# Pooled sums of v over 112 and 32 keys instead of 72 and 72, and a new hand-written order of all steps

## The chip, the cores and the metric

The kernel runs on one core of a Trainium2 chip. The metric is the device time in microseconds of one execution. Three runs of the kernel before gave 593.35, 593.8 and 591.56 us; the median is 593.35 us.

## The reference

Two stages. Attention over 8 batches of 8 heads, 576 positions of width 64, is the sum of a pooled and a local part; its result is the input of a feed-forward stage over 4608 tokens (512 to 1024 to 512). All is float32.

```python
# pooled: means of 4 neighbours, so 144 pooled queries, keys and values per head
q_d, k_d, v_d = (t.reshape(B, H, 144, 4, D).mean(axis=3) for t in (q, k, v))
out_up = np.repeat(softmax(scale * q_d @ k_d.T) @ v_d, 4, axis=2)
# local: each position sees positions less than 4 away
out_local = softmax(where(|i - j| < 4, scale * q @ k.T, -1e9)) @ v
x = (out_up + out_local).transpose(0, 2, 1, 3).reshape(4608, 512)
# feed-forward
h = x @ w_in
solu = h * softmax(h)
ln = (solu - mean(solu)) / sqrt(var(solu) + 1e-6) * g_ln
out = ln @ w_out
```

## The kernel before

The work is cut into 2039 numbered steps. A step is a stretch of a generator up to its next `yield`, mostly one to twelve instructions on one engine. The list `plan` holds them in a natural order; the string `ORDER` is a permutation of 0 to 2038 written out by hand, and the kernel issues the steps in that order. Each engine runs its instructions strictly in the order in which they are issued, so `ORDER` sets the queue of every engine, SyncE's with its DMAs too. The string `OTHER` lists the steps that go to the second of two engines: `engine(usual, instead)` returns `instead` if the step's number is in it.

The steps, by item:

- `warm` (24 steps, L1042): two matmuls on a constant tile, into the bank that the output of the feed-forward uses later. They only keep TensorE busy.
- Batches 0 and 1 (`EarlyBatch.pair_steps`): TensorE turns q and k around (L556), a copy (L262 or L264), and VectorE sums four neighbours (L418: `qd_flat`, `kd`). Batches 2 to 7 (`Batch.pair_steps`): VectorE transposes (L462, L466) and sums.
- `pooled_vload` and `pooled_vsum`: four loads per batch, each of four heads and half of the pooled keys: 288 positions as 72 partitions of 4 positions each (`vs`, L315), and two additions that make 72 pooled keys in `vd` (L486, L489). They run on GpSimd, or on VectorE for steps in `OTHER`.
- `Pooled` (32 items of 10 steps, one for each pair of heads of a batch): scores (L787), maximum (L794), exponentials (L802), division (L809, L811), twelve transposes of the probabilities by TensorE (L822, into `pdt`: a 64x72 block is the stationary operand, a 64x64 identity is streamed), two copies into `pdT`, the product with `vd` (L843), and the addition into x (L577). The two halves of the 144 keys are `kc` 0 and 1.
- `Local` and `PairOfLocals`: the local part, windows of 64 positions (L606, L694, L654, L664, L752; VectorE L624 to L642 and L700 to L745).
- `Weights.piece` (16 items): w_in and w_out arrive as float64 and are turned into two float32r parts each (L363 to L411).
- For each of 36 tiles of 128 tokens: `xhl` splits x into two parts (L1016, L1019); `ffn_in` makes h by 24 matmuls in two steps (L861), then maximum (L869), exponential (L873), product (L876), mean and spread; `ffn_back` writes u to DRAM and reads it back in blocks; `ffn_ut` transposes and splits it (L962, L968, L971); `ffn_out` makes the output by 24 matmuls in two steps (L985), scales (L992) and stores it (L994). h has one buffer of two PSUM banks and the output one bank, so tile i+1 may start h only after L876 of tile i has read it.

"h of tile 8" below means the first of the two `ffn_in` steps of tile 8 with L861. `PairOfLocals` and the steps in between are placed by `ORDER` alone; no code weighs them at run time.

Of the kernel before, what the change touches and what calls it, by code (L numbers as in the profile page):

```python
# [10 lines left out]
F32 = mybir.dt.float32  # L11
# [125 lines left out]
def pooled_local_attention_then_solu_ffn(  # L137
# [11 lines left out]
    P = 128  # L149
# [17 lines left out]
    starts = [0] + [58 * w - 3 for w in range(1, 9)] + [S - W]  # L167
    qlo = [58 * w for w in range(9)] + [520]
    qhi = qlo[1:] + [S]

    QC = 3
    QN = SD // QC

# [981 lines left out]
```

## Time and profile before

| what | value |
|---|---|
| median of three runs | 593.35 us |
| span of the profiled execution, first to last instruction | 592.8 us |
| TensorE matmul busy | 568.5 us (96%) |
| VectorE busy | 468.1 us (79%) |
| ScalarE busy | 335.9 us (57%) |
| GpSimd busy | 317.8 us (54%) |
| moved by DMA | 99.58 MB |

The profile is one execution; its span is 0.55 us below the median of the three runs. "Busy" is the share of time in which an engine had an instruction in work; TensorE's matmuls overlap one another and their ends are modelled. A line number such as L861 is the line of the kernel before.

### The profile page before, as it was taken

The page shows a single profiled execution, that of the slowest core. Times are in us where ns is not written, and L with a number is a line of the kernel's source. Part 1 is how long each engine was busy: PE and PEld are TensorE (multiplying, and loading weights), DVE is VectorE, ACT ScalarE, POOL GpSimd, SP SyncE. Part 2 cuts the span into 40 slices and gives each one's busy share as a digit, 9 for nine tenths or more (in the row PEclk, how much of TensorE's full clock was granted, in tenths as well). Part 3 has the DMA queues.
Part 4 walks back from the last instruction along what each step waited for, and adds up shares of the span by engine and source line. Part 5 has one row for each costly group of instructions (what it writes and reads, how often), then busy time and mean ns, then how long its engine had stood idle before and what let it go on. Part 6 is the DMA issues. An engine that isn't in the chain of part 4 may idle for free.

```text
span 592.8 us, 15179 instructions
## 1 busy us (share of the span) xinstructions
PE 568.5 (96%) x5832; PEld 439.3 (74%) x5832; DVE 468.1 (79%) x769; ACT 335.9 (57%) x751; POOL 317.8 (54%) x465
## 2 busy tenths in 40 slices
PE   8789799999989999999999999999999999999996
PEld 5567567677767777777777777787787777778885
DVE  6987999999898989887988968978885854654441
ACT  3577677785555655574457455575445645434443
POOL 2475799577765735485366734354532676242211
PEclk9698999999999999999999999999999999999999
DMA  9998779777787688785897858765535454332331
GB/s 272 237 239 168 162 178 201 184 143 210 178 190 179 147 235 183 173 209 169 194 187 186 203 155 156 214 150 177 159 101 159 133 143 139 106 126 90 124 108 53
DMA packets 207112, 99.58 MB, mean 168 GB/s; under 512 B 163136, under 2 KB 193344, under 8 KB 207040
## 3 DMA queue, kind: packets, MB, share of 16 engines
q1 hardware_dynamic: 207040, 98.61, 66.5%
q8 instruction: 46, 0.75, 0.6%
q14 instruction: 26, 0.21, 0.1%
HBM read 65.54 MB, written 27.79 MB: 157 GB/s over the span
## 4 chain that ended last, share of the span: by engine, by line
PE 72%; DVE 10%; SPq 4%; DMA 4%; issue 4%; POOL 3%; ACT 2%; DVEq 0%; POOLq 0%; ACTq 0%
PE h L861 28%; PE o L985 27%; SPq L285 3%; PE sd L787 2%; PE po L843 2%; PE xp L752 2%; PE pdt L822 2%; PE kp L556 2%; PE warm L1042 2%; PE qp L556 1%; PE sc L694 1%; DMA qm<-in_q_dram 1%; DMA u<-e 1%; POOL xl L1019 1%; PE sc L606 1%
## 5 line engine op out<-in xcount | busy, mean ns | idle before, releaser
L861 PE MATMUL h<-wi_h,xh 128*128 128x512 f32 x288 | 116.6, 405 | 0.9 <-DVE e L876 0.7
L985 PE MATMUL o<-wo_h,uh 128*128 128x512 f32 x288 | 116.4, 404 | 0.8 <-ACT uh L968 0.7
L861 PE MATMUL h<-wi_h,xl 128*128 128x512 f32 x288 | 114.3, 397 | 2.6 <-DVE xl L1019 1.4
L985 PE MATMUL o<-wo_l,uh 128*128 128x512 f32 x288 | 113.9, 395 | 0.0
L861 PE MATMUL h<-wi_l,xh 128*128 128x512 f32 x288 | 113.8, 395 | 0.0
L985 PE MATMUL o<-wo_h,ul 128*128 128x512 f32 x288 | 79.0, 395 | 0.0
L869 DVE TENSOR_REDUCE nmx<-h 128x1 f32<-128x1024 f32 x36 | 43.5, 1209 | 36.0 <-PE h L861 36.0
L873 ACT ACTIVATE e<-h,nmx 128x1024 f32<-128x1024 f32 x36 | 40.1, 1113 | 49.8 <-DVE nmx L869 46.0
L861 PEld LDWEIGHTS h<-wi_h,xl 128*128 128x128 f32 x288 | 54.1, 188 | 16.8 <-POOL xl L1019 2.0
L861 PEld LDWEIGHTS h<-wi_h,xh 128*128 128x128 f32 x288 | 54.1, 188 | 16.0 <-DVE e L876 1.9
L985 PEld LDWEIGHTS o<-wo_h,uh 128*128 128x128 f32 x288 | 54.0, 188 | 15.8 <-issue 1.6
L985 PEld LDWEIGHTS o<-wo_h,ul 128*128 128x128 f32 x288 | 54.0, 188 | 13.3 <-DVE ul L971 0.3
L861 PEld LDWEIGHTS h<-wi_l,xh 128*128 128x128 f32 x288 | 54.1, 188 | 12.0
L985 PEld LDWEIGHTS o<-wo_l,uh 128*128 128x128 f32 x288 | 54.1, 188 | 11.9
L971 POOL TENSOR_TENSOR ul<-v,uh 128x512 fp32r<-128x512 f32 x37 | 48.3, 1312 | 24.7 <-ACT uh L968 20.9
L876 DVE SCALAR_TENSOR_TENSOR e<-h,e 128x1024 f32<-128x1024 f32 x36 | 43.7, 1213 | 16.7 <-ACT e L873 16.5
L968 ACT ACTIVATE uh<-v 128x512 fp32r<-128x512 f32 x70 | 42.5, 623 | 21.0 <-DVE v L962 16.9
L962 DVE STREAM_TRANSPOSE v<-v 128x512 f32<-128x512 f32 x70 | 46.6, 688 | 4.8 <-DMA v<-u 4.8
L992 ACT ACTIVATE osb<-o,s 128x512 f32<-128x512 f32 x36 | 24.6, 682 | 43.3 <-PE o L985 18.3
L1019 POOL TENSOR_TENSOR xl<-x,xh 128x512 fp32r<-128x512 f32 (+1 forms) x31 | 37.6, 1219 | 16.5 <-ACT xh L1016 16.0
L881 POOL TENSOR_SCALAR nmu<-su 128x1 f32<-128x1 f32 x36 | 9.8, 273 | 67.0 <-DVE e L876 56.7
L899 ACT ACTIVATE e<-e,nmu 128x1024 f32<-128x1024 f32 x29 | 33.3, 1148 | 19.7 <-POOL nmu L881 19.7
(122 smaller groups left out, 1142.6 us busy)
## 6 DMA issues: line engine op xcount, KB each, us to landing
u<-e SPq DMA_DIRECT2D x35, 512.0 KB
v<-u SPq DMA_DIRECT2D x140, 128.0 KB
vs<-in_v_dram SPq DMA_DIRECT2D x32, 288.0 KB
out_dram<-osb SPq DMA_DIRECT2D x36, 256.0 KB
qm<-in_q_dram SPq DMA_DIRECT2D x96, 72.0 KB
km<-in_k_dram SPq DMA_DIRECT2D x96, 72.0 KB
vw<-in_v_dram SPq DMA_DIRECT2D x80, 64.0 KB
vw<-in_v_dram SPq DMA_DIRECT2D x40, 128.0 KB
```

The costliest lines, as they stand in the source:

```text
L285: nc.sync.dma_start(t[nm][Q * 32:Q * 32 + 32, pr], src[b, 2 * pr + par, :, dh * 32:dh * 32 + 32].rearrange("(k t) d -> t k d", t=32),)
L861: nc.tensor.matmul(hps[:, n, :], src[:, cc, :], wt[:, cc, n * 512:(n + 1) * 512], start=(cc == 0 and src is xh and wt is wi_h), stop=(cc = ...
L869: nc.vector.tensor_reduce(out=nmx, in_=hf, op=ALU.max, axis=AX.X, negate=True)
L873: nc.scalar.activation(e, hf, AF.Exp, bias=nmx, scale=1.0, accum_out=se)
L876: nc.vector.scalar_tensor_tensor(out=e, in0=hf, scalar=1.0, in1=e, op0=ALU.mult, op1=ALU.mult, accum_out=su)
L899: nc.scalar.activation(e, e, AF.Identity, bias=nmu, scale=1.0)
L962: nc.vector.transpose(vg, vg)
L968: nc.scalar.activation(uh, tp, AF.Copy)
L971: (usual if v is None else engine(usual, nc.vector)).tensor_tensor(out=ul, in0=tp, in1=uh.bitcast(F32), op=ALU.subtract)
L985: nc.tensor.matmul(o, src[:, j, :], wt[:, 4 * g + j, :], start=(g == 0 and j == 0 and src is uh and wt is wo_h), stop=(g == 1 and j == 3 a ...
L992: nc.scalar.activation(osb, o, AF.Copy, scale=s)
L1019: engine(nc.gpsimd, nc.vector).tensor_tensor(out=l, in0=src, in1=h.bitcast(F32), op=ALU.subtract)
```

## The change

The 144 pooled keys are cut at 112 (`K0`) instead of 72. Keys 0 to 111 lie on partitions 0 to 111 of `vd[:, 0]`; keys 112 to 143 lie on partitions 96 to 127 of `vd[:, 1]`, and partitions 0 to 95 there are set to zero once, by GpSimd. The loads of v are 112 and 32 partitions high (448 and 128 KB), the additions likewise. The twelve transposes of a `Pooled` item take 128 columns instead of 72: columns 0 to 127 for the first piece and 16 to 143 for the second, whose columns 16 to 111 meet the zeros of `vd`. The copies move the same number of elements per partition on 128 instead of 72 partitions; the products with `vd` contract over 112 and 128 partitions instead of 72. `vd` is one tile for all batches; it was a tile of a pool with one buffer. Code for a way of summing v on TensorE that was switched off (`SUMS_ON_PE = 0`) is removed. The plan of 2039 steps and their numbers stay as they are; `ORDER` is a new permutation of them, and `OTHER` has 118 numbers instead of 115.

```diff
 ORDER = """
-23 16 165 166 2 4 167 168 169 170 171 24 26 27 25 28 29 3 172 33 32 30 31 173 174 197 17 175
...
+12 3 18 173 24 26 174 8 17 165 166 25 175 176 177 178 27 15 179 167 168 169 2 28 170 29 32 30 31
...
+    K0 = 112
...
+    KEYS = ((0, slice(0, K0), slice(0, K0)), (SD - P, slice(K0, SD), slice(P - SD + K0, P)))
+    vd = cpool.tile([P, 2, H, D], F32, name="vd")
+    nc.gpsimd.memset(vd[0:P - SD + K0, 1], 0.0)
+
     def load_vs(b, c, hs):
-        vs = big(f"vs_{b}_{c}_{hs.start}")[0:72].rearrange("p (h x) -> p h x", h=H // 2)
+        _, keys, at = KEYS[c]
+        vs = big(f"vs_{b}_{c}_{hs.start}")[at].rearrange("p (h x) -> p h x", h=H // 2)
         nc.sync.dma_start(
-            vs, v[b, hs, c * 288:(c + 1) * 288, :].rearrange("h (p t) d -> p h (t d)", t=FAC)
+            vs, v[b, hs, FAC * keys.start:FAC * keys.stop, :].rearrange(
+                "h (p t) d -> p h (t d)", t=FAC
+            ),
         )
...
         def value(self, kc, head):
-            return [self.vd[:, kc, head, :]]
+            return [vd[0:(K0, P)[kc], kc, head, :]]
...
-                out=self.vd[:, c, hs], in0=vs[:, :, 0:D], in1=vs[:, :, D:2 * D], op=ALU.add
+                out=vd[KEYS[c][2], c, hs], in0=vs[:, :, 0:D], in1=vs[:, :, D:2 * D], op=ALU.add
...
-            pt = pt[0:72, :, 0:2 * QC * 64].rearrange("p x (k j n) -> p x k j n", k=2, j=QC)
+            pt = pt[:, :, 0:2 * QC * 64].rearrange("p x (k j n) -> p x k j n", k=2, j=QC)
...
-                            pt[:, x, kc, j, :], pd[rows(x), (0, 2, 1)[c], kc * 72:(kc + 1) * 72],
+                            pt[:, x, kc, j, :], pd[rows(x), (0, 2, 1)[c], KEYS[kc][0]:KEYS[kc][0] + P],
                             ident[rows(x), rows(x)],
...
-            pdT = wk.tile([72, 2, QC, 2, QN], F32, tag="pdT", name=f"pdT_{b}_{pr}")
+            pdT = wk.tile([P, 2, QC, 2, QN], F32, tag="pdT", name=f"pdT_{b}_{pr}")
...
                         nc.tensor.matmul(
-                            po[par * 64:par * 64 + 64, :], vt, pdT[:, kc, par * SD:(par + 1) * SD],
+                            po[par * 64:par * 64 + 64, :], vt,
+                            pdT[0:(K0, P)[kc], kc, par * SD:(par + 1) * SD],
```

More of the change, by code (lines that the diff above doesn't have):

```diff
@@ L179, in pooled_local_attention_then_solu_ffn @@
     WARM = 24
-    SUMS_ON_PE = 0
     G_LATE = False
@@ L224, in pooled_local_attention_then_solu_ffn @@
     nc.vector.memset(mhalf, -0.5)
-    GR = SD // 2
-    BAND = {0: (0, 16), 1: (3, 15), 3: (1, 15)}
-    bands = {}
-    def make_bands():
-        t = moe.tile([P, DFF], F32, tag="e", name="bands")[:, 0:3 * 160]
-        t = t.rearrange("p (r x) -> p r x", r=3)
-        nc.gpsimd.memset(t, 0.0)
-        by_half = ident.rearrange("p (h k) -> p h k", h=2)
-        for n, (r, (off, m)) in enumerate(BAND.items()):
-            nc.vector.tensor_reduce(
-                out=t[:, n, GR:GR + m],
-                in_=by_half[:, :, off:off + FAC * m].rearrange("p h (j i) -> p j h i", i=FAC),
-                op=ALU.add, axis=AX.XY,
-            )
-            bands[r] = t[:, n]
     LP = 2 * W + 2
@@ L439, in __getattr__ @@
                 self.kd = att.tile([P, NPR, SD], F32, tag="kd", name=f"kd_{self.b}", bufs=2)
-            elif what == "vd":
-                self.vd = att.tile([72, 2, H, D], F32, tag="vd", name=f"vd_{self.b}")
             else:
@@ L489, in pooled_vsum @@
             eng.tensor_tensor(
-                out=self.vd[:, c, hs], in0=vs[:, :, 0:D], in1=vs[:, :, D:2 * D], op=ALU.add
+                out=vd[KEYS[c][2], c, hs], in0=vs[:, :, 0:D], in1=vs[:, :, D:2 * D], op=ALU.add
             )
-        def pool_steps(self):
-            firsts = [-(-s0 // FAC) for s0 in starts]
-            ends = firsts[1:] + [SD]
-            for c in range(2):
-                tp = two_banks(ps_h, "h", f"vp_{self.b}_{c}")[0:GR]
-                at = tp.rearrange("p h (r a d) -> p h r a d", r=NPR, a=2)
-                ws = range(5 * c, 5 * c + 5)
-                for w in ws:
-                    s0, g0, g1 = starts[w], firsts[w], ends[w]
-                    at0 = GR - (g0 - GR * c)
-                    K = FAC * g1 - s0
-                    for half in range(2):
-                        nc.tensor.matmul(
-                            at[:, half, :, half ^ (w % 2), :],
-                            bands[s0 % FAC][half * W:half * W + K, at0:at0 + GR],
-                            self.vw[w // 2][half * W:half * W + K, w % 2],
-                            start=w == ws[0], stop=w == ws[-1],
-                        )
-                yield
-                vd = self.vd[:, c].rearrange("p h d -> p (h d)")
-                nc.scalar.activation(vd, tp[:, 0], AF.Copy)
-                yield
-                nc.vector.tensor_tensor(out=vd, in0=vd, in1=tp[:, 1], op=ALU.add)
-                yield
     class EarlyBatch(Batch):
@@ L1076, in attention @@
     def attention(bt):
-        by_pe = bt.b < SUMS_ON_PE
         late = bt.b == 0
@@ L1083, in attention @@
         pooled = [Pooled(bt, pr, late) for pr in range(NPR)]
-        if by_pe:
-            if not bt.b:
-                step(make_bands)
-            for u in range(5):
-                step(bt.load_v, u)
-            row(bt.pool_steps(), 6)
-        else:
-            values(bt)
+        values(bt)
         for it in pooled + local if late else local + pooled:
@@ L1097, in attention @@
                 continue
-            if isinstance(it, Local) and not by_pe:
+            if isinstance(it, Local):
                 step(bt.load_v, it.u)
```

202 rows, old and new, of tables (ORDER, OTHER) are left out of this document.

## The prediction, made before the changed kernel was run

> **What bounds the kernel now.** I read the page's busy totals first, then the chain that ended last, then busy time by stage. Columns of a stage: stretch and length in us, then busy us of TensorE's matmuls, its weight loads, VectorE, ScalarE and GpSimd with the instructions of each, granted clock, DMA share, GB/s.
>
> ```profile
> PE 568.5 (96%) x5832; PEld 439.3 (74%) x5832; DVE 468.1 (79%) x769; ACT 335.9 (57%) x751; POOL 317.8 (54%) x465
> ...
> PE 72%; DVE 10%; SPq 4%; DMA 4%; issue 4%; POOL 3%; ACT 2%; DVEq 0%; POOLq 0%; ACTq 0%
> ```
>
> ```profile
> 0.00:60.00 60.00, 49.77 (x778) 36.19 (x782) 48.24 (x88) 35.94 (x92) 29.24 (x36) 0.86 0.96 228
> 60.00:185.10 125.10, 116.82 (x1530) 87.96 (x1519) 119.48 (x202) 83.85 (x190) 92.53 (x109) 1.00 0.79 180
> 185.10:592.80 407.70, 401.90 (x3540) 315.15 (x3540) 300.41 (x481) 216.15 (x471) 196.04 (x321) 1.00 0.59 155
> ```
>
> ```profile
> 183.92 0.80 DVE e L876
> 185.07 3.07 PE h L861 x12
> ...
> 194.01 5.60 PE o L985 x24
> 199.61 5.60 PE h L861 x24
> ```
>
> 96% says TensorE, but the stages differ. Up to 185.1 us VectorE has the upper hand: between 60 and 185.1 us it is busy 119.48 of 125.1 us, and the chain (start, length, engine, result, line) steps from VectorE to TensorE at h of tile 8. From there the chain is almost TensorE alone, with 401.90 of 407.7 us busy. So the time is two sums: when h of tile 8 or 9 can start (VectorE's work ahead of it plus VectorE's holes), and TensorE's work from there to the end. VectorE's holes before 185.1 us are 11.76 + 5.62 = 17.4 us. Loads matter at the start, where the DMA engines are 0.96 busy; later at 0.59 to 0.79 they are not the bound.
>
> **The transposes of the probabilities.** Each of the 32 `Pooled` items has twelve; their stationary operand grows from 72 to 128 columns. Rows: line, engine, result and operands, weights by moving tile, count, then busy us and mean ns of one.
>
> ```profile
> L822 PE MATMUL pdt<-ident,pd 64*72 64x64 f32 x384 | 16.9, 224 | 0.0
> ...
> L654 PE MATMUL plt<-ident,pl 128*128 128x128 f32 x80 | 12.9, 283 | 2.2 <-POOL pl L644 1.5 <-ACT plT L262 0.7
> ...
> L822 PEld LDWEIGHTS pdt<-ident,pd 64*72 64x72 f32 x384 | 12.1, 113 | 8.9 <-issue 6.2 <-ACT pl L635 0.4 <-DVE pl L700 0.4
> ...
> L654 PEld LDWEIGHTS plt<-ident,pl 128*128 128x128 f32 x80 | 8.7, 140 | 5.4 <-POOL pl L644 2.3 <-issue 1.0 <-POOL s L925 0.8
> ```
>
> ```profile
> 205.14 0.86 PE L822 MATMUL pdt<-ident,pd 64*72 64x64 f32 x24
> 205.93 0.66 PE L654 MATMUL plt<-ident,pl 128*128 128x128 f32 x4
> 206.34 0.48 PE L985 MATMUL o<-wo_h,uh 128*128 128x512 f32 x1
> ```
>
> A load of 128 columns takes 140 ns, one of 72 takes 113: 27 ns more. The second view gives starts: 24 transposes fill 205.14 to 205.93, 0.79 us, so 33 ns each or 66 ns for two, less than load plus matmul of one. Two run side by side (the two 64-row halves), and within a half load and matmul follow each other; the 128-column transposes of L654, which use the whole array, take 0.41 us for four, 102 ns each. Per column loaded or streamed that is 102/256 = 0.40 ns there and at most 66/136 = 0.49 ns here, so 56 more columns are 22 to 27 ns for a pair. I take 27 ns a pair: 6 pairs, 0.16 us an item. In the new order 20 of the 32 items have their transposes after the start of h of tile 9, where TensorE is the bound: 20 x 0.16 = 3.2 us. Ends: 0, if the loads hide behind other matmuls, and 20 x 12 x 0.027 = 6.5 us, if pairs stop overlapping. The other 12 items lie where TensorE has idle time (8.28 us between 60 and 185.1); without that cover they would add 12 x 0.16 = 1.9 us. That TensorE then starts the product later by 0.16 us makes only the copies late, which wait for nothing else.
>
> The page "TensorE: Matmul & The Clock Gate" of the Trainium skill, section "LDWEIGHTS (loading the stationary operand)", says that a load takes its number of columns divided by 1.2 per ns, whatever its rows. That would be 47 ns more for 56 columns; the two rows above show 27, so the trace does not bear the page's slope. By the page the 20 items would cost 20 x 6 x 0.047 = 5.6 us instead of 3.2.
>
> **The rest of the edit, each off the path.** Contraction over 112 and 128 instead of 72 rows, and tiles with more partitions:
>
> ```profile
> L486 POOL TENSOR_TENSOR vs<-vs 72x512 f32<-72x512 f32 x24 | 32.4, 1350 | 0.5 <-DMA vs<-in_v_dram 0.3
> L1019 POOL TENSOR_TENSOR xl<-x,xh 128x512 fp32r<-128x512 f32 x23 | 31.8, 1384 | 14.2 <-ACT xh L1016 13.9 <-issue 0.2
> ...
> L843 PE MATMUL po<-pdT,vd 72*64 72x144 f32 x256 | 22.8, 299 | 0.4 <-ACT x L262 0.4
> L787 PE MATMUL sd<-kd,qd_flat 64*64 64x144 f32 x384 | 21.9, 299 | 3.2 <-DVE pl L624 1.8 <-DVE kd L418 1.4
> ...
> masks.py:197 POOL MEMSET ident<- 128x128 f32 x1 | 0.2, 205 | 0.3 <-POOLq L1137 0.3
> ```
>
> ```profile
> 10.00:15.00 5.00, 4.94 (x72) 3.09 (x68) 3.79 (x7) 2.35 (x4) 0.00 (x0) 1.00 1.06 323
> ```
>
> The same 144 columns take 299 ns with 64 and with 72 rows, so I take zero for more rows; at worst 2%, the scatter of such means, on the 20 products after tile 9. GpSimd takes 1350 ns for 512 elements on 72 partitions and 1384 on 128: at most 34 ns, zero as GpSimd is off the path; the copies, with equal elements per partition, likewise. The one memset is four times the elements of the 205 ns one, at most 0.8 us, in a GpSimd queue that does nothing between 10 and 15 us. `vd` had one buffer and has one, so no new wait for it; if zeroing came late, the first product would wait, and that is after 30 us.
>
> **The new order.** All steps move, so I count, for both orders, what each queue has ahead of a start of h and what TensorE has left after it, each step at the mean of its row. TensorE's steps from h of tile 9 on are the same in kind and number in both: 54 and 60 halves of h and o, 20 transposes and 20 products of `Pooled`, 17 of its scores, 14 and 36 steps of the local part. VectorE's steps through the last one that h of tile 8 needs: 252 steps, 179.4 us before; 247 steps, 175.5 us after. Through the last one that h of tile 9 needs: 270 steps, 191.9 us, and 269 steps, 191.0 us. (These sums run above VectorE's busy time, 48.24 + 119.48 = 167.7 us by 185.1, because neighbours overlap in the records; both orders are counted alike.) Rows of the larger differences:
>
> ```profile
> L418 DVE TENSOR_REDUCE kd<-kT 128x144 f32<-128x576 f32 x32 | 23.5, 736 | 3.7 <-ACT kT L262 3.5
> ...
> L462 DVE STREAM_TRANSPOSE kT<-km 128x576 f32<-128x576 f32 x24 | 18.0, 757 | 0.0
> ...
> L486 DVE TENSOR_TENSOR vs<-vs 72x512 f32<-72x512 f32 x8 | 7.0, 877 | 0.0
> ...
> L264 DVE COPY x<-xp 128x464 f32<-128x464 f32 x11 | 6.9, 629 | 1.5 <-PE xp L752 1.5
> ...
> L489 DVE TENSOR_TENSOR vd<-vs 72x256 f32<-72x256 f32 x8 | 6.3, 788 | 0.3
> ```
>
> By tile 9 the new order has two more transposes (L462) and two more sums (L418) for later batches, 3.0 us, and three fewer copies (L264) and no addition of v on VectorE (L486 with L489), 3.6 us; smaller ones balance to -0.3. The other queues ahead of tile 9: GpSimd 110 steps in both, ScalarE 177 before and 183 after, SyncE 256 DMAs before and 249 after. ScalarE's six more steps lie beside 41 us of its idle time between 60 and 185.1.
>
> Before, h of tile 8 starts at 185.1, so 5.7 us above its VectorE sum; for tile 9 that gives 191.9 + 5.7 = 197.6, and the chain shows 199.6, since TensorE needs 199.61 - 185.07 = 14.5 us between the two. After, with the same 5.7 us: tile 8 at 181.2, tile 9 by TensorE at 195.7 and by VectorE at 191.0 + 5.7 = 196.7. The later counts: 2.9 us earlier than 199.6. VectorE's row at tile 9 is what is late next.
>
> **Sum.** -2.9 + 3.2 = +0.3 on the span of 592.8: 593.1 us. The profiled execution lies 0.55 us below the median of the runs, 593.35, so 593.7 us. A difference under 0.5%, 3.0 us, is about what a measurement of this kernel cannot tell from none.
>
> **Rival 1: VectorE's holes at the start close (faster).** The holes stand in brackets, with what ended them:
>
> ```profile
> 5.16 0.43 DVE L365 TENSOR_SCALAR w<-w 128x512 f32<-128x512 f32 x1 [2.02 <-ACT w L363]
> 8.68 0.76 DVE L264 COPY qT<-qp 128x576 f32<-128x576 f32 x1 [1.17 <-PE qp L556]
> 11.28 0.75 DVE L418 TENSOR_REDUCE kd<-kT 128x144 f32<-128x576 f32 x1 [1.06 <-ACT kT L262]
> 30.87 0.69 DVE L624 TENSOR_TENSOR pl<-sc,mask 128x512 f32<-128x512 f32 x1 [0.61 <-PE sc L606]
> 33.67 0.69 DVE L624 TENSOR_TENSOR pl<-sc,mask 128x512 f32<-128x512 f32 x1 [0.80 <-PE sc L606]
> 49.47 0.75 DVE L418 TENSOR_REDUCE kd<-kT 128x144 f32<-128x576 f32 x1 [2.03 <-ACT kT L262]
> 54.02 0.61 DVE L794 TENSOR_REDUCE mxd<-sd 128x3 f32<-128x432 f32 x1 [1.44 <-PE sd L787]
> ```
>
> The first is the wait for the first weights and stays. The other six are 7.1 us; four end with TensorE, two with ScalarE's copy of TensorE's result. The new order puts two pieces of weights ahead of the first sum, and two more `warm` steps ahead of the third pair of heads. If 5 of the 7.1 us go, everything after moves by as much: 588.7 us. Against it: the DMA engines are 0.96 busy there, and the first k now comes behind a second weights load of 512 KB. From 3.4 us on it decides for faster.
>
> ```profile
> vs<-in_v_dram SPq DMA_DIRECT2D x32, 288.0 KB
> ```
>
> Two pages would feed this rival; the row above is the loads of v that the second bears on. The same page's "Part 1: The HAM clock gate" says that TensorE runs at half clock until a window of about 3.4 us was busy, and again after an idle one; the mean clock of 0.86 in the first 60 us agrees. "DMA: Bandwidth & Descriptors" of the Trainium skill, section "Why a DMA increments its semaphore by 16 and not by 1", says that a load uses the largest number of engines up to 16 that divides its rows: 12 for 72, 16 for 112 or 32; no row here shows the engines of one load. By it, the first batch's four loads, 1.18 MB, would take 25 KB off the fuller engines, at 228/16 GB/s some 1.7 us, an estimate from that page.
>
> **Rival 2: the holes grow (slower).** VectorE's queue is in order; a step that now stands ahead of its input stops all behind it, and TensorE through them. Place: before tile 9, where 17.4 us of holes are to be kept at the same size by an order in which every neighbour is new. If they grow by a quarter, 4.4 us, the time is 598.1; from 2.6 us on it decides for slower. For it: only 5.62 us of holes in 125 us after 60 us, so almost any late input shows. Against it: the queue ahead of tile 8 is 3.9 us shorter.
>
> **Rival 3: the pairs of transposes stop overlapping (slower).** 6.5 instead of 3.2 us: 597.0; it decides from 24 ns per transpose. Against it: nothing in their order on TensorE changes.
>
> **How the numbers follow.** Forecast 0.42, rival 1 0.30, rival 2 0.18, rival 3 0.10. Faster is rival 1: 0.30. Slower is rivals 2 and 3: 0.28. Same: 0.42, with a range of its own of 590.4 to 596.3. The range for 8 in 10 goes from rival 1 at 588.7 to past rival 2, 588.3 to 599.0.
>
> **What would show it.** Right: the transposes' load near 140 ns and 24 of them in about 1.1 us; h of tile 9 starting at 196 to 198 us; from there to the end about 396 us (393.2 before), with TensorE as full as before. Wrong: h of tile 9 before 193 us (rival 1) or after 200 us (rival 2), or the stretch after it longer than 398 us (rival 3, or a hole in the late part that the counts do not see).

## The result, and the profile after

The changed kernel takes 598.97 us (median of 20 runs, 595.62 to 602.3), the kernel before, measured beside it on the same chip, 593.21 us (20 runs, 589.98 to 597.99). The ratio is 1.0094, with a 95% interval of 1.0072 to 1.0117: 0.9% slower, some 5.6 us. The forecast was no change that can be measured (593.7 us), with 590.4 to 596.3 as the range of that outcome; the time is outside it, on the side to which the prediction gave 0.28. It is inside the wide range, 588.3 to 599.0, by 0.03 us, and that is luck: single executions of the changed kernel go from 595.62 to 602.3 us. Ratios, and the medians in the table of the experiments, leave out executions in a slower state of the chip.

The page of the changed kernel, busy totals and the chain's shares by engine:

```profile
PE 573.1 (96%) x5832; PEld 442.0 (74%) x5832; DVE 469.8 (79%) x769; ACT 334.4 (56%) x752; POOL 319.0 (53%) x465
...
PE 73%; DVE 13%; ACT 3%; issue 3%; DMA 3%; SPq 2%; POOL 2%; DVEq 0%; ACTq 0%; POOLq 0%
```

TensorE is 96% busy as before, but with 573.1 instead of 568.5 us of it for as many instructions. In the chain VectorE's share is 13% instead of 10%. The stages of the changed kernel (columns as in the prediction; h of tile 8 starts at 185.6, of tile 9 at 199.4 us, here and below counted from its first weight load, some 0.2 us ahead of its first matmul, from which the prediction counts):

```profile
0.00:60.00 60.00, 48.31 (x769) 33.53 (x772) 47.11 (x83) 35.62 (x90) 30.48 (x37) 0.89 0.96 227
60.00:185.60 125.60, 120.12 (x1550) 91.96 (x1541) 116.72 (x199) 85.22 (x194) 91.10 (x111) 0.97 0.78 178
185.60:596.50 410.90, 404.65 (x3530) 316.54 (x3528) 306.01 (x488) 213.54 (x470) 197.45 (x317) 1.00 0.58 155
199.40:596.50 397.10, 390.90 (x3442) 305.87 (x3440) 293.06 (x467) 203.07 (x443) 187.75 (x307) 1.00 0.57 154
```

The last stage of the kernel before, from its own h of tile 9:

```profile
199.20:592.80 393.60, 387.80 (x3442) 304.18 (x3440) 288.03 (x462) 206.85 (x449) 186.97 (x306) 1.00 0.59 156
```

**Where the time went in the two traces.** VectorE's work ahead of h of tile 8 is as much shorter as counted: 47.11 + 116.72 = 163.83 us busy, against 48.24 + 119.48 = 167.72 before, 3.9 us less. Yet h of tile 8 starts at 185.6, not 181.2: VectorE's holes grew from 17.4 to 21.8 us (11.8 to 12.9 in the first 60 us, 5.6 to 8.9 after): 4.4 more holes less 3.9 of work is the 0.5 us by which h of tile 8 is later.

That sum is book-keeping; it does not say what h of tile 8 waits for. Before, its wait ends with VectorE (`e`, L876). In the changed kernel it waits for nothing. The chain passes from ScalarE to TensorE at 119.2 us (first rows), and from there TensorE works without a gap, 66.36 of 66.40 us, until h of tile 8 is the next in its queue; in the same stretch of the kernel before (the row between) it has 2.5 us of gaps:

```profile
118.58 0.61 ACT pdT L245 x2
...
119.24 0.71 PE sd L750 x12
```

```profile
119.20:185.10 65.90, 63.41 (x685) 49.03 (x683) 60.99 (x101) 39.87 (x91) 43.70 (x61) 1.00 0.77 179
```

```profile
119.20:185.60 66.40, 66.36 (x749) 51.92 (x749) 59.57 (x99) 42.06 (x102) 43.95 (x63) 1.00 0.79 178
```

So 6.8 of VectorE's 21.8 us of holes lie where TensorE sets the pace. They hold up nothing that h of tile 8 waits for; the last of them is itself a wait for TensorE:

```profile
185.69 0.75 DVE L540 TENSOR_TENSOR x<-x,po 128x576 f32<-128x576 f32 x1 [1.52 <-PE po L806]
```

From h of tile 9 to the end the changed kernel takes 397.1 us, the kernel before 393.6: 3.5 us more, with 3.1 us more of TensorE's busy time for the same 3442 matmuls.

In the runs of the two kernels the time is the span plus 1.7 to 1.9 us. If the stage from h of tile 9 takes the same in all runs of a kernel, the median puts that start at 598.97 - 1.8 - 397.1 = 200.1 us after, and at 593.21 - 1.8 - 393.6 = 197.8 before. That is an estimate: 2.3 us of the loss lie ahead of tile 9 and 3.5 behind it.

VectorE's larger holes at the start of the changed kernel (its timeline; the bracket is the idle time before the instruction, and what ended it):

```profile
9.08 0.43 DVE L355 TENSOR_SCALAR w<-w 128x512 f32<-128x512 f32 x1 [1.52 <-ACT w L353]
...
13.50 0.75 DVE L408 TENSOR_REDUCE kd<-kT 128x144 f32<-128x576 f32 x1 [1.41 <-ACT kT L245]
...
30.32 0.75 DVE L408 TENSOR_REDUCE qd_flat<-qT 128x144 f32<-128x576 f32 x1 [1.42 <-ACT qT L245]
...
38.20 0.61 DVE L757 TENSOR_REDUCE mxd<-sd 128x3 f32<-128x432 f32 x1 [2.38 <-PE sd L750]
...
41.11 0.69 DVE L587 TENSOR_TENSOR pl<-sc,mask 128x512 f32<-128x512 f32 x1 [1.03 <-PE sc L569]
```

The holes that rival 1 counted at 49.47 and 54.02 us are gone, but five of 1.0 to 2.4 us stand here, ended by ScalarE or TensorE. Ahead of the largest stands another stall: sd follows in TensorE's queue on a product (po) in the middle of which TensorE stood still at 33.0, with nothing in the trace that it waits for (TensorE's timeline; the second row is the rest of the same product):

```profile
32.54 0.46 PE L806 MATMUL po<-pdT,vd 112*64 112x144 f32 x3
35.19 0.98 PE L806 MATMUL po<-pdT,vd 112*64 112x144 f32 x5 [2.19 <-issue]
```

Three of the four other kernels below with this order stand still at the same place: 0.87 us in e1, 1.81 in e3, 1.78 in e11.

### The profile page after: what moved, and what is told of

It reads as the page before. It is cut to its first block, busy times and chain, and to the rows that moved or that the text cites. A ratio compares the mean times of both kernels' runs of the same rounds, so it can differ in the third digit from the quotient of the medians.

```text
span 596.5 us, 15236 instructions
## 1 busy us (share of the span) xinstructions
PE 573.1 (96%) x5832; PEld 442.0 (74%) x5832; DVE 469.8 (79%) x769; ACT 334.4 (56%) x752; POOL 319.0 (53%) x465
## 4 chain that ended last, share of the span: by engine, by line
PE 73%; DVE 13%; ACT 3%; issue 3%; DMA 3%; SPq 2%; POOL 2%; DVEq 0%; ACTq 0%; POOLq 0%
PE o L949 28%; PE h L825 28%; PE po L806 2%; PE sd L750 2%; DMA qm<-in_q_dram 2%; PE pdt L785 2%; PE xp L715 2%; PE sc L657 2%; SPq L268 1%; PE warm L1006 1%; PE sc L569 1%; DVE e L840 1%; DVE nmx L833 1%; PE xp L627 1%; DVE w L368 1%
## 5 line engine op out<-in xcount | busy, mean ns | idle before, releaser
L825 PE MATMUL h<-wi_h,xh 128*128 128x512 f32 x288 | 117.9, 409 | 0.9 <-DVE e L840 0.9
L935 POOL TENSOR_TENSOR ul<-v,uh 128x512 fp32r<-128x512 f32 x43 | 57.5, 1338 | 47.8 <-ACT uh L932 34.1
L932 ACT ACTIVATE uh<-v 128x512 fp32r<-128x512 f32 x70 | 43.2, 626 | 35.4 <-DVE v L926 22.3
L949 PEld LDWEIGHTS o<-wo_l,uh 128*128 128x128 f32 x288 | 54.1, 188 | 11.8
L245 ACT ACTIVATE pdT<-pdt 128x288 f32<-128x288 f32 x48 | 18.0, 410 | 43.7 <-PE pdt L785 31.0
L882 ACT ACTIVATE e<-e 128x1024 f32<-128x1024 f32 x35 | 36.8, 1050 | 3.4 <-DMA u<-e 3.3
```

Source lines behind the costliest of these rows:

```text
L245: nc.scalar.activation(out, in_, AF.Copy)
L825: nc.tensor.matmul(hps[:, n, :], src[:, cc, :], wt[:, cc, n * 512:(n + 1) * 512], start=(cc == 0 and src is xh and wt is wi_h), stop=(cc = ...
L882: nc.scalar.activation(e0, e, AF.Square, accum_out=m2)
L932: nc.scalar.activation(uh, tp, AF.Copy)
L935: (usual if v is None else engine(usual, nc.vector)).tensor_tensor(out=ul, in0=tp, in1=uh.bitcast(F32), op=ALU.subtract)
L949: nc.tensor.matmul(o, src[:, j, :], wt[:, 4 * g + j, :], start=(g == 0 and j == 0 and src is uh and wt is wo_h), stop=(g == 1 and j == 3 a ...
```

## The experiments

A table of all kernels that bear on order and pieces. "h9" is the start of h of tile 9 in the profiled execution, "rest" the time from there to the last instruction. "T" is where the chain ahead of h of tile 8 is TensorE's alone from; for the old order that is h of tile 8 itself, which waits for VectorE. "Holes" are VectorE's ahead of h of tile 8. Each ratio is against the kernel before on the same chip; the kernel before took 593.21 us on the first, 593.07 beside e1 to e4, 594.12 beside e7 and e8 and 594.54 beside e11 and e12, so that kernels are compared by ratios, not by medians.

| kernel | order | pieces, columns of a transpose | median us | ratio, 95% interval | holes | T | h9 | rest |
|---|---|---|---|---|---|---|---|---|
| before | old | 72/72, 72 | 593.21 | 1 | 17.4 | 185.1 | 199.2 | 393.6 |
| changed | new | 112/32, 128 | 598.97 | 1.0094 [1.0072, 1.0117] | 21.8 | 119.2 | 199.4 | 397.1 |
| e1_order_only | new | 72/72, 72 | 602.16 | 1.0136 [1.0094, 1.0177] | 17.3 | 118.1 | 197.3 | 397.7 |
| e2_pieces_only | old | 112/32, 128 | 591.42 | 0.9972 [0.9953, 0.9992] | 17.9 | 181.9 | 196.1 | 393.5 |
| e3_new_order_64_80 | new | 64/80, 80 | 602.85 | 1.0146 [1.0107, 1.0186] | 22.4 | 124.5 | 203.7 | 396.4 |
| e4_old_order_64_80 | old | 64/80, 80 | 594.24 | 1.0029 [1.0002, 1.0056] | 21.1 | 188.3 | 202.4 | 393.6 |
| e7_old_order_80_64_wide | old | 80/64, 128 | 591.80 | 0.9993 [0.9956, 1.0029] | 16.3 | 183.5 | 197.7 | 393.5 |
| e8_old_order_32_112 | old | 32/112, 112 | 591.55 | 0.9961 [0.9934, 0.9989] | 13.0 | 180.2 | 194.3 | 392.8 |
| e11_tail | new, one step moved | 112/32, 128 | 599.30 | 1.0076 [1.0047, 1.0105] | 21.5 | 118.4 | 198.6 | 396.3 |
| e12_fill_idle | new, ten fillers more | 112/32, 128 | 598.75 | 1.0063 [1.0032, 1.0095] | 20.2 | 118.3 | 198.5 | 396.2 |

Two things stand out. All five kernels of the new order have TensorE alone on the chain from 118.1 to 124.5 us on, and from there to the end they take 475.6 to 477.3 us: what differs between their traces lies ahead of T. And VectorE's holes scatter in one and the same order, from 13.0 to 21.1 us in the old and from 17.3 to 22.4 in the new, as does its busy time (163.3 to 167.7 us; e1, the new order, has 166.3 and e2, the old, 164.1). These are single executions, so the 4.4 us of holes and the 3.9 us of work of the first pair can't be put down to the order by that pair alone.

**One half of the change at a time: e1_order_only and e2_pieces_only.**

```diff
# e1: the kernel before, with the new permutation
-ORDER = """ 23 16 165 166 2 4 ...      OTHER = (115 numbers)
+ORDER = """ 12 3 18 173 24 26 ...      OTHER = (118 numbers)
# e2: the changed kernel, with the old permutation
-ORDER = """ 12 3 18 173 24 26 ...      OTHER = (118 numbers)
+ORDER = """ 23 16 165 166 2 4 ...      OTHER = (115 numbers)
```

> The kernel before with the new ORDER and OTHER alone; pieces of 72 and 72 and transposes of 72 columns stay. Theory A (most of the loss is the order): about 4 us over the kernel before, 597 us. Theory B (most of the loss is the 128-column transposes and the pieces): within 1.5 us of the kernel before, 592 to 594.5 us.

> The changed kernel with the ORDER and OTHER of before: pieces of 112 and 32, 128-column transposes. Theory A: the transposes' spacing, 66 instead of 57 ns a pair in the trace of the changed kernel, gives 0.06 us an item and 1.2 us on 20 items behind h of tile 9, up to 1.9 us on all 32: 594 to 595.5 us. Theory B: 4 to 6 us over the kernel before, 597 to 599 us.

Measured: the order alone is 1.4% slower, the pieces alone 0.3% faster. Theory A is right about which half is slow, but both times lie past what it gave (597 us, and 594 to 595.5). The last stage of both (busy us by stage, from h of tile 9):

```profile
197.30:595.00 397.70, 390.08 (x3442) 304.60 (x3441) 294.77 (x467) 202.81 (x443) 187.45 (x307) 1.00 0.59 154
```

```profile
196.10:589.60 393.50, 388.61 (x3442) 305.75 (x3440) 290.27 (x462) 206.84 (x449) 184.58 (x306) 1.00 0.57 156
```

So the loss is the order's. In the last stage it shows in all five traces of the new order (rest 396.2 to 397.7 us, against 392.8 to 393.6 in the old); ahead of tile 9 it rests on the estimate above, since e1's profiled execution, the shortest of its six, has h9 at 197.3 us. The wider transposes seem to add nothing to the last stage, 393.5 us with 128 columns in the old order against 393.6 with 72, but they do: TensorE's time on them behind tile 9 (first in each row) is 10.19 us before and 11.32 in e2, and 10.39 in e1 and 11.55 in the changed kernel, 1.1 to 1.2 us more in either order.

```profile
199.20:592.80 393.60, 10.19 (x240) 7.38 (x240) 7.53 (x18) 8.23 (x22) 1.00 0.59 156
```

```profile
196.10:589.60 393.50, 11.32 (x240) 8.85 (x240) 7.59 (x18) 8.33 (x22) 1.00 0.57 156
```

What hides them in e2 is that the trace of the kernel before has a wait of TensorE that e2's has not:

```profile
478.32 0.50 PE L861 MATMUL h<-wi_h,xl 128*128 128x512 f32 x1 [0.94 <-POOL xl L1019]
```

e8, whose transposes have 112 columns and take 10.54 us, has 392.8 us. In the time the pieces take 0.28% off in the old order (1.7 us) and by the ratios 0.42% in the new, where the two intervals overlap.

**Is it the number of keys in a piece? e3_new_order_64_80 and e4_old_order_64_80.** 64 and 80 are both multiples of 16, as 112 and 32 are; transposes of 80 columns.

```diff
-    K0 = 112
-    KEYS = ((0, slice(0, K0), slice(0, K0)), (SD - P, slice(K0, SD), slice(P - SD + K0, P)))
+    K0, KW = 64, 80
+    KEYS = ((0, slice(0, K0), slice(0, K0)), (K0, slice(K0, SD), slice(0, SD - K0)))
```

> The changed kernel with pieces of 64 and 80 keys and transposes of 80 columns (columns 0 to 79 and 64 to 143; keys 64 to 79 of the first piece meet zeros), new order. Heights are still multiples of 16. Theory A: the transposes nearly at their old price, so 1 us under the changed kernel, 597.5 to 598.5 us. Theory B: 4 us or more under it, 593 to 595 us.

> Pieces of 64 and 80 keys, transposes of 80 columns, with the ORDER and OTHER of before. If heights that are multiples of 16 make the loads of v land sooner and that moves the start, 590 to 592 us. If the loads are hidden anyway, the kernel before within 1 us: 592.5 to 594 us.

Measured: neither is better than 72 and 72 in the same order (1.0146 against 1.0136; 1.0029 against 1). e3 missed both of its theories. The rest repeats by order: 396.4 and 393.6 us. If the rule of the Trainium skill's page "DMA: Bandwidth & Descriptors", section "Why a DMA increments its semaphore by 16 and not by 1", were what makes 112/32 better, 64/80 would gain as well. It does not; these runs don't bear the rule out as the cause.

**What of the pieces, then? e7_old_order_80_64_wide and e8_old_order_32_112.** The first has nearly equal pieces with the wide transposes, the second the unequal pieces the other way round with 112 columns.

```diff
# e7
-    K0 = 112
+    K0 = 80
# e8
-    K0 = 112
-    KEYS = ((0, slice(0, K0), slice(0, K0)), (SD - P, slice(K0, SD), slice(P - SD + K0, P)))
+    K0, KW = 32, 112
+    KEYS = ((0, slice(0, K0), slice(0, K0)), (K0, slice(K0, SD), slice(0, SD - K0)))
```

> Old order, pieces of 80 and 64 keys with 128-column transposes. Two theories for why 112 and 32 gave 591.5 us and 64 and 80 gave 594.7 in the same order. Wide: the 128-column transposes help (they keep TensorE's clock up): then 591 to 592.5 us here too. Unequal: the piece of 32 keys, 128 KB, lands sooner: then as 64 and 80, 594 to 595.5 us.

> Old order, pieces of 32 and 112 keys with 112-column transposes (columns 0 to 111 and 32 to 143). Unequal: 591 to 592.5 us if any small piece helps; if it must be the second one that is small, as the old order needs it to be, 593 to 595. Wide: near 592, since the transposes are nearly as wide.

Measured: 32/112 gains as 112/32 does, 80/64 lies between them and no gain. Both times fit "wide" as they stand, but the kernel before took 594.12 us beside them, so the ratios count. Unequal pieces go with the gain in both kernels that have them; the intervals of 80/64 and of the two overlap, so that is as far as it goes. Why it helps is open. e2 and e8 are the two versions that beat both kernels.

**The order cut in two: e5_new_ramp and e6_old_ramp.** Pieces of 112 and 32; the steps up to h of tile 9 from one order, the remaining ones in the sequence of the other. `OTHER` is put together in the same way (110 and 121 numbers).

```diff
# e5: 822 steps of the new order, then what is left in the old sequence
# e6: 817 steps of the old order, then what is left in the new sequence
# in outline: ORDER = the first part, then the steps of the other order that are not in it
```

> Pieces of 112 and 32. New ORDER up to the first half of h of tile 9 (822 steps), the other 1217 steps in the order of before. The pieces alone gave 591.5 us, the whole change 599.0. If the new order loses in both stages (traces: about 3.5 us after h of tile 9, the rest before), 595 to 596.5 us, and from h of tile 9 to the end as in the old order, 393.5 us. If it loses in the ramp alone, 598 to 599.

> Pieces of 112 and 32. ORDER of before up to the first half of h of tile 9 (817 steps), the other 1222 steps in the new order. If both stages lose: 594.5 to 595.5 us, with about 397 us from h of tile 9 to the end. If the late stage only looked longer because of what the ramp left behind: 591.5 to 592.5.

Measured: 606.52 us, ratio 1.02 [1.0145, 1.0254], and 604.59 us, 1.0185 [1.0144, 1.0226]. Both expectations missed: both hybrids are slower than either whole order. One wait of TensorE behind the seam shows why, e5 first and e6 below it:

```profile
209.92 1.11 PE L613 MATMUL plt<-ident,pl 128*128 128x128 f32 x4 [5.96 <-POOL pl L603]
```

```profile
208.56 0.79 PE L945 MATMUL o<-wo_h,uh 128*128 128x512 f32 x1 [8.09 <-ACT osb L952]
```

TensorE stands still for 6.0 and 8.1 us until one step of GpSimd and one of ScalarE are done. From h of tile 9 to the end the two take 401.3 and 406.6 us. Without these waits that is 395.3 with the old sequence and 398.5 with the new: an estimate, since what a wait holds up may have had slack, but on the same side as the whole orders (393.6 and 397.1). On the stage ahead of tile 9 the hybrids say nothing.

**What in the new order costs 3 us behind tile 9.** From the starts of TensorE's matmuls between h of tile 9 and h of tile 35 I summed the time from each matmul to the next, apart for neighbours of the same operation and of different ones. Same operation: 332.1 us before and 332.2 after, equal by chance: the wider transposes add 1.0 us, and the wait at 478.32 us of the kernel before is not there. Different ones: 32.7 us (167 places) before, 32.7 in e2, and 35.4 us (165 places) after. By kind of place, count and mean us:

| from one operation to another | before | e2 | changed |
|---|---|---|---|
| from h or o to another | 36 x 0.325 | 36 x 0.325 | 40 x 0.326 |
| back to h or o | 36 x 0.152 | 36 x 0.151 | 40 x 0.176 |
| between h and o | 29 x 0.234 | 29 x 0.233 | 26 x 0.262 |
| among the others | 66 x 0.132 | 66 x 0.133 | 59 x 0.144 |

A matmul of h or o is followed by its like after 0.233 us, so leaving them costs 0.09 and returning up to 0.15. The new order leaves h and o forty times where the old does it thirty-six times: 4 x (0.326 + 0.152) = 1.9 us, less 3 x 0.234 and 7 x 0.132 for the fewer places of the other kinds: 0.3 us. The remaining 2.4 us are the higher means, in three of the four rows. Some 1.3 us of them are three waits of h and o for ScalarE or VectorE, of which this is the longest (the others, 0.15 and 0.24 us, at 260.13 and 415.57 us):

```profile
254.10 0.50 PE L949 MATMUL o<-wo_h,uh 128*128 128x512 f32 x1 [0.47 <-ACT osb L956]
```

The others are dearer neighbours: one and the same pair of operations has the same median in both traces within 0.01 us (back to h or o 0.15 us from a transpose or a local score, 0.21 from a pooled score or product), but the new order has more of the dear pairs. To see whether a change of kind has a price of its own:

**e9_wide_dummies and e10_small_dummies.** The kernel of e2, with two matmuls more between the halves of h of 27 tiles; they differ only in the part of the array that these use.

```diff
         for n in range(2):
+            if n == 1 and i >= 9:
+                for x in range(2):      # M = 128 in e9, 64 in e10
+                    nc.tensor.matmul(
+                        hps[0:M, 1, x * 64:x * 64 + 64], ident[0:M, 0:M], ident[0:M, 0:64],
+                        start=True, stop=True,
+                    )
```

> Pieces of 112 and 32 keys in the order of before, and between the two halves of h of tiles 9 to 35 two dummy matmuls of the whole array (128 x 128 stationary, 64 columns moved), written to a part of the bank that the second half overwrites. The output is unchanged. This is the control for the next kernel: the same number of added matmuls, no change of kind. A whole-array transpose of 128 columns takes 102 ns here, so two of half as many columns cost 0.1 to 0.2 us a tile: 27 tiles, 3 to 5 us more than the same kernel without them (591.5 us median): about 595.5.

> As the control, but the two dummy matmuls use a 64 x 64 block of the array, so each of 27 tiles has two more changes of kind (whole array to block and back). Theory (a change of kind makes TensorE wait until the array is empty): by the spacings of the traces, h to a 64 x 64 block costs 0.326 instead of 0.233 us and a block to h 0.148 us, so 27 x (0.09 + 0.15) = 6.5 us more than the matmuls by themselves; the blocks themselves take less than 0.05 us each, so 4 us over the control and 7 to 9 over the kernel without dummies: 599 to 600. Rival (the larger share of changes in the new order is a matter of which waits fall there, and a change itself is free): not slower than the control, since each dummy is smaller.

Measured: 602.56 us, ratio 1.0133 [1.0096, 1.0171], and 606.41 us, 1.0201 [1.0159, 1.0242]. Against e2's ratio the control cost 1.6%, some 10 us, not 3 to 5, so both times lie past what was expected; the small ones cost 3.9 us more than the control on the same chip, as expected (4). One place of each, in the timeline of TensorE, e9 and then e10:

```profile
288.52 0.40 PE L831 MATMUL h<-wi_h,xl 128*128 128x512 f32 x1
288.75 0.55 PE L825 MATMUL h<-ident 128*128 128x64 f32 x4
289.12 0.48 PE L831 MATMUL h<-wi_h,xh 128*128 128x512 f32 x1
```

```profile
292.18 0.39 PE L831 MATMUL h<-wi_h,xl 128*128 128x512 f32 x1
292.50 0.44 PE L825 MATMUL h<-ident 64*64 64x64 f32 x4
292.87 0.51 PE L831 MATMUL h<-wi_h,xh 128*128 128x512 f32 x1
```

Four records are two matmuls in two passes each. In e9 the four start 0.23 after the last h, as another h would, and h is back 0.37 later. In e10 they start 0.32 after the last h, and h is back 0.37 later, though one starts only 0.058 us after the other (0.111 in e9). The last stages of the two:

```profile
195.90:601.60 405.70, 400.85 (x3550) 317.94 (x3548) 291.08 (x462) 206.98 (x449) 183.81 (x306) 1.00 0.56 151
```

```profile
199.00:607.10 408.10, 403.24 (x3550) 312.12 (x3548) 291.69 (x462) 207.00 (x449) 184.05 (x306) 1.00 0.55 150
```

408.1 against 405.7 us: 2.4 us more for dummies whose own starts (0.107 + 0.058 + 0.058, against 0.056 + 0.111 + 0.111 us) take 1.5 us less over 27 tiles. So 54 changes of kind cost some 3.9 us, 0.07 each, an estimate from one trace of each: the rival, a free change, is out. The section "Key Properties" of the Trainium skill's page "TensorEngine Tiling (Array Packing)" says that a change of the tiling mode makes the engine drain; these runs agree as far as the price goes, the drain itself they do not show. It is shown that the price exists; that the four more visits are what the order loses by is not, for their part is 0.3 us by the table and the rest are dearer neighbours and waits.

**The last tile: e11_tail.** The new order issues ScalarE's copy of u of tile 35 ahead of its copy of the output of tile 34, and the output of tile 35 uses the same bank.

```diff
-... 2004 2029 2030 2031 2014 2032 2015 ...
+... 2004 2029 2030 2014 2031 2032 2015 ...
```

> The changed kernel with one step moved: the copy of the output of tile 34 on ScalarE goes ahead of its copy of u for tile 35, as in the order of before. Theory: the stretch from the transposes of u of tile 35 to the first output matmul falls from 1.6 to about 0.96 us, and h of tile 35 to the end from 29.3 to 28.6 us; in the time 0.65 us, less than these runs can tell from none. Rival (something else holds the output there): the stretch stays at 1.6 us.

The end of the chain, before, changed, and e11:

```profile
581.42 0.89 PE ut L958 x8
582.99 5.89 PE o L985 x24
```

```profile
584.42 0.89 PE ut L922 x8
585.89 0.69 ACT osb L956
586.62 5.88 PE o L949 x24
```

```profile
583.81 0.69 ACT osb L952
585.11 5.88 PE o L945 x24
```

Before, the output (o) starts 0.68 us after the transposes of u end (581.42 + 0.89); after, it waits 1.31 us, and the wait ends with osb. In e11 the output waits 0.69 us, for uh as before; from the start of the last transpose to the output it is 0.96 us again, 1.6 without the edit. From h of tile 35 to the end it takes 28.4 us, 29.0 without the edit and 28.4 before. The theory holds at its place; 0.65 us of the 3.5 is shown. The time of the whole, 1.0076 against 1.0094, can't show it.

**The clock at the start: e12_fill_idle.**

```diff
-        for _ in range(2):
+        for _ in range(2 if n else 12):
             nc.tensor.matmul(
```

> The changed kernel with twelve filler matmuls instead of two in the step that stands ahead of TensorE's longest idle stretch (18.7 to 21.9 us), after which its granted clock was 0.5 until 27.6. Theory A (half-clock stretches at the start are part of the loss): that stretch at half clock goes, VectorE's holes before h of tile 8 fall by 1 to 3 us, and the time is 1 to 3 us less than the changed kernel's 599.0: 596 to 598. Theory B (the holes belong to the order; the clock is only their consequence): the clock improves there, but h of tile 8 still starts at 185 us or later and the time is within 1 us of 599.0. The stall that came at the 350th matmul (33.0 us, 2.2 us long) should, if it is tied to the count, come twenty matmuls of the sequence earlier, among the local scores, and not at the product.

Two stretches of the start, the changed kernel and then e12 (the granted clock stands third from the end):

```profile
20.00:28.00 8.00, 6.01 (x63) 4.93 (x64) 7.54 (x11) 3.92 (x12) 4.34 (x4) 0.57 0.85 158
34.00:42.00 8.00, 6.81 (x117) 4.96 (x119) 4.51 (x9) 4.46 (x14) 4.14 (x4) 0.57 1.05 232
```

```profile
20.00:28.00 8.00, 6.81 (x114) 4.99 (x114) 7.90 (x12) 4.82 (x14) 5.71 (x5) 1.00 0.85 175
34.00:42.00 8.00, 5.59 (x125) 4.62 (x116) 7.83 (x17) 5.78 (x16) 3.88 (x4) 1.00 1.12 248
```

Ten fillers in one idle stretch took both stretches from 0.57 to full clock, the second (34 to 42 us) too. h of tile 0 starts at 62.6 instead of 67.3 us, a lead of 4.7. But h of tile 8 starts at 184.7 instead of 185.6: 0.9 us of the lead is left. The ratio is 1.0063 [1.0032, 1.0095], where the changed kernel has 1.0094 [1.0072, 1.0117]. That would be 1.8 us less, as in theory A, but the intervals overlap, so the time does not decide between the theories. The clock alone is not what the new order lost by: in the first 60 us the kernel before has an even lower mean than the changed one (0.86 against 0.89), from there to h of tile 8 a higher one (1.00 against 0.97). VectorE in e12:

```profile
0.00:60.00 60.00, 48.83 (x819) 32.67 (x822) 49.82 (x90) 37.89 (x94) 33.20 (x39) 0.97 0.97 228
60.00:184.70 124.70, 115.80 (x1511) 88.10 (x1503) 114.69 (x191) 82.51 (x190) 88.15 (x110) 1.00 0.77 178
```

Its holes are 10.2 us in the first 60 (12.9 in the changed kernel) and 10.0 from there to h of tile 8 (8.9), 20.2 in all instead of 21.8: the start did close by 2.7 us. The lead is still 4.1 us at the first output and 0.9 us at h of tile 3, and from 118.3 us on TensorE works without a gap, as in the changed kernel from 119.2. In between, VectorE in e12, and the same instruction in the changed kernel:

```profile
98.89 3.58 DVE L364 SCALAR_TENSOR_TENSOR w<-w,w 128x512 int32<-128x512 int32 x1
```

```profile
102.57 0.86 DVE L364 SCALAR_TENSOR_TENSOR w<-w,w 128x512 int32<-128x512 int32 x1
```

3.58 instead of 0.86 us: 2.7 of the 3.2 us given back. It is counted as busy time. GpSimd in e12 meanwhile:

```profile
98.39 1.28 POOL L935 TENSOR_TENSOR ul<-v,uh 128x512 fp32r<-128x512 f32 x1
99.63 1.04 POOL L607 TENSOR_TENSOR pl<-pl,rsl 128x512 f32<-128x512 f32 x1
100.63 1.29 POOL L401 TENSOR_TENSOR wo_l<-w,wo_h 128x512 fp32r<-128x512 f32 x1
```

GpSimd has three operations back to back until 101.92, and VectorE's ends 0.55 us after that, about its usual 0.69. In e1 and e3 the same instruction took 3.34 and 4.74 us, and there and in the changed kernel, too, it ends 0.55 to 0.56 us after the end of a GpSimd operation (at 100.72, 107.07 and 102.88 us). In the kernels of the old order no instruction of this kind took more than 1.8 us. The Trainium skill's page "SBUF — State Buffer", section "SBUF: two separate sides", says that VectorE with two operands in SBUF and GpSimd share a pair of ports under an exclusive lock, and that the loser is blocked altogether; the times agree, and no run here changes that neighbourhood alone. The stall at the product did not come twenty matmuls earlier: 0.41 us at the same product, now ending with the sum of v at 31.12 us. That it is tied to a count is refuted; what it waited for in the changed kernel is open.

## Why the prediction came out as it did, by its steps

- **"when h of tile 8 or 9 can start (VectorE's work ahead of it plus VectorE's holes)"**: this is the step that failed. It holds in the old order, where h of tile 8 waits for VectorE. In the new one TensorE works without a gap from 118.1 to 124.5 us on, in all five kernels, and h of tile 8 stands behind some 66 us of TensorE's own work. The prediction counted every other queue ahead of tile 9, but TensorE's only behind it. So the term of -2.9 us for an earlier h of tile 9 measured +0.15 us in the two traces (199.60 against 199.45 us, by the first matmul) and +2.3 by the estimate for the medians.
- **"with the same 5.7 us"**: h of tile 8 stands 10.1 us above its VectorE sum, 4.4 more. That is the price of rival 2 to the digit, and luck for the most part: 1.1 us of the growth lie in the first 60 us and 1.3 between 60 and 119.2, where VectorE can hold TensorE up, and 1.9 behind that, where it is an effect. In other executions the same holes are 17.3 us in the new order and 21.1 in the old. Rival 2's mechanism, steps ahead of their inputs, is seen in part (the five holes above); what sets the 118 to 124 us from which TensorE is full is not shown.
- **VectorE's work ahead of h of tile 8** ("3.9 us shorter"): 163.83 against 167.72 us, as counted; but e1, the same steps in the same order with the old pieces, has 166.3, so the agreement is no proof of the count.
- **"the same in kind and number"** for TensorE's steps from h of tile 9: true, and the conclusion, the same time, false. Who stands next to whom and three waits cost 2.7 us, and one step at the end 0.65 (e11). I had compared numbers of steps and not their sequence.
- **The transposes, +3.2 us**: the load came out at 143 ns (140 expected), but a pair starts 66 ns after the last instead of 57, 9.5 more and not 27. The rows and a place with the transposes of two items:

```profile
L474 POOL TENSOR_TENSOR vs<-vs 112x512 f32<-112x512 f32 (+1 forms) x25 | 33.5, 1339 | 6.2 <-DMA vs<-in_v_dram 5.1
...
L806 PE MATMUL po<-pdT,vd 112*64 112x144 f32 (+1 forms) x256 | 23.5, 302 | 3.2 <-issue 2.2 <-DVE x L540 0.6 <-ACT x L245 0.3
...
L785 PE MATMUL pdt<-ident,pd 64*128 64x64 f32 x384 | 19.0, 236 | 3.3 <-DVE pd L774 3.3
...
L785 PEld LDWEIGHTS pdt<-ident,pd 64*128 64x128 f32 x384 | 14.8, 143 | 11.2 <-issue 5.0 <-ACT smd L769 3.7 <-POOL vs L474 0.4
```

```profile
208.09 0.96 PE L785 MATMUL pdt<-ident,pd 64*128 64x64 f32 x24
208.98 0.66 PE L617 MATMUL plt<-ident,pl 128*128 128x128 f32 x4
```

  208.09 to 208.98 is 0.89 us where 0.79 stood, not 1.1. All transposes behind tile 9 take 1.1 to 1.2 us more, in both orders, a good third of the term. It was mis-sized by 2.0 us: of the 30 ns that a load is longer, 9.5 show in the spacing of a pair. Rival 3 is out. The estimate by the slope of the Trainium skill's page "TensorE: Matmul & The Clock Gate", section "LDWEIGHTS (loading the stationary operand)", 47 ns for 56 columns and 5.6 us in all, is further off still: the rows show 30 ns.
- **From h of tile 9 to the end "about 396 us"**: 396.9 from the first matmul, nearly right for the wrong reason, as the transposes' term was too large and the order's was missing. By the prediction's own signs neither "right" (h of tile 9 at 196 to 198 us) nor "wrong" (after 200 us, or a stretch over 398 us) came about.
- **The edits at nothing**: right. The products took 302 ns (299 before) with 112 and 128 rows, GpSimd's additions 1339 ns on 112 and 32 partitions (1350), ScalarE's copies 410 (400).
- **The profiled execution lies "0.55 us below the median"**: wrong, the span was compared with a time. The execution took some 594.6 us, 1.2 above the median. The forecast is the median plus the 0.3 us of the sum either way.
- **Rival 1**: two of its six holes closed, others opened; in e12 the start closed by 2.7 us and a lead of 4.7 us at h of tile 0 was 0.9 at h of tile 3 and of tile 8.

The chance of 0.28 for slower was too low for what the prediction itself knew: between 60 and 185.1 us VectorE's slack was 5.6 us and TensorE's 8.3, every neighbour was new, and the forecast gain rested on VectorE alone. The part that does gain, the pieces in the old order (0.9972), was not seen at all: it was costed as +3.2 us.

## What to carry to other kernels

A count of the work ahead of a start gives the least time, not the time; count it for every queue that leads there, the busiest engine's own too, since a new order can change which of them comes last. When all neighbours change, put a price of its own on the holes, and let the old ones be no forecast. Where an engine with one queue is full, count its changes of kind as well as its instructions, and follow the last tile step by step. Try the parts of a change apart: here the order cost 1.4% and hid a gain of 0.3% from the pieces, why they gain is open, and the version to keep is the old order with 112 and 32 (or 32 and 112) keys.

## What the runs showed of the hardware that I had not expected

- TensorE going from h or o to a smaller kind takes 0.326 us to the next start instead of 0.233, and a change of the part of the array in use costs some 0.07 us (e9 against e10).
- A two-pass matmul of the whole array with 64 columns costs 0.11 us for each pass. Two of them cost 12.2 us over 27 tiles in the last stage (405.7 against 393.5), 0.45 us a tile: nearly the two matmuls of h that would fit there.
- One idle stretch of TensorE of 3.3 us was followed by 6.8 us at half clock, and filling it changed a second such stretch 13 us later as well; of the 4.7 us saved at h of tile 0, 0.9 reached h of tile 8.
- A VectorE instruction of 0.69 us took 3.3 to 4.7 us beside three or four operations of GpSimd back to back in three kernels and ended 0.55 us after one of them, all recorded as busy: holes in brackets are not all that an engine loses.
